# Two PSUM banks set apart for the gate products, smaller stores of the normalised rows, and an earlier start of two stages

## The chip, the core and the metric

The kernel runs on one core of one Trainium2 chip. The metric is the device time of one execution in microseconds (us). The profile comes from one more execution of the same program, taken by the hardware profiler; "unit", "slot" and "step" below are words of this kernel and are explained with it.

## What is computed

Eight sequences of 3008 tokens with 256 channels are filtered in the frequency domain (a real FFT along the tokens, a product with a complex filter, the inverse FFT). Each token is then normalised by its root mean square and goes through a SwiGLU feed-forward layer of width 1536:

```python
X = np.fft.rfft(x, axis=1)
y = np.fft.irfft(X * (filt_r + 1j * filt_i)[None], n=x.shape[1], axis=1)
t = y.reshape(8 * 3008, 256)
xn = t / np.sqrt(np.mean(t * t, axis=-1, keepdims=True) + 1e-6) * rms_g
g = xn @ w_gate
out = (g / (1 + np.exp(-g)) * (xn @ w_val)) @ w_out
```

## The kernel before

**The feed-forward layer** is the frame of the kernel. The tokens of a batch are cut into chunks (eight chunks of 376 tokens for batch 0, five of 512 and one of 448 for each of batches 1 to 7), and the hidden width into 12 tiles of 128. One chunk and one tile make a *unit*; there are 96 units for batch 0 and 72 for each later batch. `unit(g, jt)` multiplies the gate weights into the PSUM bank `pg` (L341, two matmuls) and the value weights into `pv` (L345, two matmuls), lets ScalarE write silu of `pg` to `sg` (L348), and lets VectorE write `pv` times `sg` to `hh` (L350). `project` follows three units behind and adds `hh` times the output weights to the two banks `po` of the chunk (L363), which are held for 12 units, then copied out and stored.

**The filter** of a batch runs in three steps that are inserted between the units by a plan written out by hand. `s1` is the first small Fourier product (bank `psa`, L144) and stores to the DRAM array `a_tmp`; `load_a2` reads it back in another order (L160). `s2` multiplies by the second table (bank `psp`, L200), and VectorE and GpSimd apply the filter (for batches 0 and 1 VectorE alone, tiles `t` at L207 and L208); `s2z` is the product back (bank `psz`, L229 and L232), copied by ScalarE to `z_sb` (L234) and stored to `z_tmp`; `load_z2` reads that back (L244). `s3` is the last product (bank `psy`, L250); ScalarE squares and sums each half of it (tile `junk`, L256), `s3r` makes the factor `rho` on GpSimd (L265, L267) one slot later, and `s3n` lets VectorE write the normalised rows to `n_sb` two slots after `s3` (L276), the last reader of `psy`. Four calls of `s3n` fill a tile that is stored to `n_tmp`; when a batch is stored, `load_xn` reads its chunks back transposed as `xn` (L318), which the units of that batch use.

Batch 0 goes ahead of the units. Its first product is turned on TensorE (`turn`, bank `psa`, L189, copied at L192), its normalised rows go by `s3n_first` (L287) and `load_xn_first`, and its first two chunks by `turn_n` (L299, L304, L306).

**The order.** `tc.manual_schedule()` keeps the order of the Python code on each engine. The main loop calls `unit(u)`, then the steps that the plan has for slot u, then `project` for unit u - 3:

```python
        for u in range(total + LAG):
            if u < total:
                unit(u // JT, u % JT)
                steps(u)
            if u >= LAG:
                project((u - LAG) // JT, (u - LAG) % JT)
```

Within a slot `s3n` and `s3n_first` come first, then `s3r`, then `s2z`, then the rest. For batch 1 `s2` starts in slot 14 with one call every three slots, `s2z` three slots behind it, and `s3` starts in slot 63 with two calls in every three slots. For batch b from 2 on `s3` starts 31 slots ahead of the batch's first unit, with four calls in every five slots. `s3` of batch 0's chunks 2 to 7 takes two slots in every eight from slot 2 to slot 43, and `s1` of batch 2 takes slots 44 to 59.

**PSUM.** All products use tiles of one bank from one pool of eight. A new tile takes a bank that is free in the program's order; its first matmul waits until the last reader of the bank's former tile is done.

**The queues.** Stores, and the loads of `a2`, `z2` and `xn`, are issued by SyncE's queue in the order of the code. `x` is loaded by GpSimd's queue.

Of the kernel before, what the change touches and what calls it, by code (L numbers as in the profile page):

```python
# [10 lines left out]
FP32 = mybir.dt.float32  # L11
FP16 = mybir.dt.float16
# [4 lines left out]
P = 128  # L17
D = 256
# [7 lines left out]
PY = 96  # L26
# [48 lines left out]
def kernel(  # L75
# [11 lines left out]
    nc = tc.nc  # L87
# [10 lines left out]
    n_dram = nc.dram_tensor("n_tmp", (B, PY, RP, D), FP16, kind="Internal").ap()  # L98
    n0_dram = nc.dram_tensor("n0_tmp", (RP // 4, PY, 4, D), FP16, kind="Internal").ap()

    glob = ctx.enter_context(tc.tile_pool(name="glob", bufs=1))
    work = ctx.enter_context(tc.tile_pool(name="work", bufs=2))
    psum = ctx.enter_context(tc.tile_pool(name="psum", bufs=8, space=bass.MemoryType.PSUM))

    def bank(name):
        return psum.tile([P, 512], FP32, tag="bank", name=name)

    w1_sb = glob.tile([PX, QZ], FP16)
    t_sb = glob.tile([QZ, PY], FP16)
# [29 lines left out]
    def s1(b, i, eng):  # L139
        v = st[b]  # L140
        if i % 4 == 0:
            v.a = work.tile([QZ, 8, D], FP16, tag="a_sb", name="a_sb", bufs=4)
        ps = bank("psa")
        nc.tensor.matmul(ps[0:QZ, :], w1_sb, v.x[i // 4][:, ds(2 * (i % 4), 2), :],  # L144
                         start=True, stop=True)
        dst = v.a[:, ds(2 * (i % 4), 2), :]
        src = ps[0:QZ, :].rearrange("p (r d) -> p r d", r=2)
        if eng == 0:
            nc.scalar.activation(out=dst, in_=src, func=AXT.Copy)  # L149
        else:  # L150
            nc.vector.tensor_copy(out=dst, in_=src)
        if i % 4 == 3:
            nc.sync.dma_start(
                a_dram[b].rearrange("s c r d -> (s c) r d")[:, ds(8 * (i // 4), 8), :], v.a)
# [8 lines left out]
    def s1_first(g):  # L163
        v = st[0]
        if g == 0:
            t1 = work.tile([P, RP, D], FP16, tag="z2", name="at", bufs=1)
            v.at = t1.rearrange("p a b -> p (a b)")[:, 0:2 * NS * P].rearrange(
                "p (h s r c) -> p h s r c", h=2, s=NS, r=RP)
            v.a2 = work.tile([P, NS, D], FP16, tag="a2", name="a2", bufs=1)
        for i in range(2):  # L170
            for dh in range(2):
                ps = bank("psa")
                for r in range(4):
                    nc.tensor.matmul(ps[:, ts(r, QZ)], v.x[g][:, 4 * i + r, ts(dh, P)], w1_sb,
                                     start=(r == 0), stop=(r == 3))
                dst = v.at[:, dh, :, ds(8 * g + 4 * i, 4), :]
                src = ps[:, 0:4 * QZ].rearrange("p (r s c) -> p s r c", r=4, s=NS)
                if dh == 0:
                    nc.scalar.activation(out=dst, in_=src, func=AXT.Copy)
                else:  # L180
                    nc.vector.tensor_copy(out=dst, in_=src)

    def turn(j):
        v = st[0]
        ps = bank("psa")
        for e in range(2):
            for dh in range(2):
                k = 2 * e + dh
                nc.tensor.matmul(ps[:, ts(k, P)],  # L189
                                 v.at[:, dh, 2 * j + e, :, :].rearrange("p r c -> p (r c)"),  # L190
                                 eye_sb, start=(k == 0), stop=(k == 3))
        nc.scalar.activation(out=v.a2[:, ts(j, 2), :],  # L192
                             in_=ps.rearrange("p (s d) -> p s d", s=2), func=AXT.Copy)
# [77 lines left out]
    def s3n(b, q):  # L271
        v = st[b]
        ps, rho = v.y.pop(q)
        if q % 4 == 0:
            v.n = work.tile([PY, 8, D], FP16, tag="n_sb", name="n_sb", bufs=2)
        nc.vector.tensor_tensor(out=v.n[:, ds(2 * (q % 4), 2), :],  # L276
                                in0=ps[0:PY, :].rearrange("p (r d) -> p r d", r=2),
                                in1=rho.unsqueeze(-1).to_broadcast([PY, 2, D]), op=ALU.mult)
        if q % 4 == 3:
            nc.sync.dma_start(n_dram[b, :, ds(8 * (q // 4), 8), :], v.n)  # L280

    def s3n_first(c):
        v = st[0]
        n = work.tile([PY, 8, D], FP16, tag="n_sb", name="n0", bufs=2)
        for k in range(2):
            ps, rho = v.y.pop(2 * c + k)
            nc.vector.tensor_tensor(out=n[:, ts(k, 2), :],  # L287
                                    in0=ps[0:PY, :].rearrange("p (r d) -> p r d", r=2),
                                    in1=rho.unsqueeze(-1).to_broadcast([PY, 2, D]), op=ALU.mult)
        if c >= PRE:  # L290
            nc.sync.dma_start(n0_dram[c], n[:, 0:4, :])
        return n

    def turn_n(c, n):
# [41 lines left out]
    def unit(g, jt):  # L336
        b, c, w = chunks[g]
        xn = st[b].xn[c]
        pg = bank("pg")
        for dt_ in range(2):  # L340
            nc.tensor.matmul(pg[:, 0:w], wg_sb[:, dt_, ts(jt, P)], xn[:, dt_, 0:w],  # L341
                             start=(dt_ == 0), stop=(dt_ == 1))
        pv = bank("pv")
        for dt_ in range(2):
            nc.tensor.matmul(pv[:, 0:w], wv_sb[:, dt_, ts(jt, P)], xn[:, dt_, 0:w],  # L345
                             start=(dt_ == 0), stop=(dt_ == 1))
        sg = work.tile([P, 512], FP32, tag="sg", name="sg", bufs=3)
        nc.scalar.activation(out=sg[:, 0:w], in_=pg[:, 0:w], func=AXT.Silu)  # L348
        hh = work.tile([P, 512], FP16, tag="hh", name="hh", bufs=5)
        nc.vector.tensor_tensor(out=hh[:, 0:w], in0=pv[:, 0:w], in1=sg[:, 0:w], op=ALU.mult)  # L350
        hh_of[(g, jt)] = hh
# [44 lines left out]
    def at(slot, f, *args):  # L396
        plan.setdefault(slot, []).append((f, args))

    for c in range(PRE, RP // 4):
        k = 2 + 8 * (c - PRE)  # L400
        at(k, s3, 0, 2 * c, 2)
        at(k + 1, s3, 0, 2 * c + 1, 2)
        at(k + 2, s3r, 0, 2 * c, 2)
        at(k + 4, s3n_first, c)
        at(k + 7, load_xn_first, c)

    for b in range(1, B):
        end = FIRST + UNITS * (b - 1)
        o_s1 = 44 if b == 2 else end - 118
        o_s2, p_s2 = (14, 3) if b == 1 else (end - 75, 2)  # L410
        o_s3 = 63 if b == 1 else end - 31
        if b > 1:
            at(o_s1 - 18, load_x, b)
            for i in range(16):
                at(o_s1 + i, s1, b, i, i % 2 if b == 2 else 0)
            at(o_s1 + 16, load_a2, b)
        for j in range(12):
            k = o_s2 + p_s2 * j
            at(k, s2, b, j)
            at(k + (3 if b < 2 else 5), s2z, b, j)  # L420
        at(k + (4 if b < 2 else 6), load_z2, b)
        for q in range(16):
            k = o_s3 + q + (q // 2 if b == 1 else q // 4)
            at(k, s3, b, q)
            at(k + 1, s3r, b, q)
            at(k + 2, s3n, b, q)
        for c in range(6):
            at(k + 3 + c, load_xn, b, c)
# [62 lines left out]
    with tc.manual_schedule():  # L491
# [20 lines left out]
        for j in range(15):  # L512
            if j < 12:
                turn(j)
            if 0 <= j - 2 < 12:
                s2(0, j - 2)
            if j in (2, 5, 8):
                copy_f(j // 3 + 1)
            if 0 <= j - 4 < 12:
                s2z(0, j - 4)  # L520
            if j == 6:
                load_w(4)
            if j == 10:
                load_x(1)
                for i in range(4):
                    fold_w(i, nc.gpsimd)
                load_wo(0)
# [12 lines left out]
        load_wo(1)  # L540
        load_wo(2)
        n0 = s3n_first(0)
        turn_n(0, n0)
        load_w(4)
        n1 = s3n_first(1)
        at(2, turn_n, 1, n1)
        load_z2(0, 16, 16)
# [5 lines left out]
# [6 lines that stand above are left out]
# [31 lines left out]
```

## Time and profile before

| | |
|---|---|
| median of 3 runs (lowest to highest) | 903.63 us (902.5 to 903.73) |
| the profiled execution's own time | 903.38 us |
| its span, first to last instruction | 901.5 us |
| granted TensorE clock, mean over the span | 0.984 |
| granted TensorE clock, first 50 us and next 50 us | 0.83 and 0.90 |
| granted TensorE clock from 100 to 850 us | 1.00 |
| ScalarE's `sg` (L348), x600 | 569 ns mean |
| VectorE's `hh` (L350), x600 | 658 ns mean |
| ScalarE's `junk` (L256), x256 | 380 ns mean, and 191 ns for reading the sum |
| VectorE's `n_sb` (L276), x112 | 677 ns mean |
| store of `n_tmp` from `n_sb`, x28 of 384 KB | 3.0 us median to landing |
| store of `n_tmp` from `n`, x6 of 192 KB | 2.5 us median to landing |
| load of `a`, x28 of 384 KB | 5.7 us median to landing |

Busy shares are averages over the span, and the ends of matmuls are modelled. So the distance from the start of one matmul to the start of the next says more about a delay on TensorE than its busy time does. In a line of the timeline the first number is the start in us from the span's start, the second is how long the row lasts; a line with "x2" holds two instructions in one. Idle time and what ended it stand in brackets. Instructions of different units overlap in a timeline, so a chain is read by going from each line to the one that it waits for.

### The profile page before, as it was taken

The page shows a single profiled execution, that of the slowest core. Times are in us where ns is not written, and L with a number is a line of the kernel's source. Part 1 is how long each engine was busy: PE and PEld are TensorE (multiplying, and loading weights), DVE is VectorE, ACT ScalarE, POOL GpSimd, SP SyncE. Part 2 cuts the span into 40 slices and gives each one's busy share as a digit, 9 for nine tenths or more (in the row PEclk, how much of TensorE's full clock was granted, in tenths as well). Part 3 has the DMA queues.
Part 4 walks back from the last instruction along what each step waited for, and adds up shares of the span by engine and source line. Part 5 has one row for each costly group of instructions (what it writes and reads, how often), then busy time and mean ns, then how long its engine had stood idle before and what let it go on. Part 6 is the DMA issues. An engine that isn't in the chain of part 4 may idle for free.

```text
span 901.5 us, 16399 instructions
## 1 busy us (share of the span) xinstructions
PE 864.4 (96%) x5528; PEld 549.9 (61%) x5528; DVE 647.1 (72%) x1025; ACT 641.4 (71%) x1455; POOL 336.7 (37%) x438
## 2 busy tenths in 40 slices
PE   5769999999999999999999999999999999999997
PEld 4436776666556655666556665566656665566655
DVE  4768887895588847797477965789477985865554
ACT  4656768677886778677886878867786775854543
POOL 3822104492245803285044821459033850500000
PEclk9869999999999999999999999999999999999999
DMA  8996665565435565344645554365653425260101
GB/s 201 243 261 149 162 163 187 119 147 140 136 101 142 127 146 170 99 109 129 161 147 129 141 126 143 107 131 144 146 159 100 96 78 116 77 130 24 43 29 45
DMA packets 140796, 117.30 MB, mean 130 GB/s; under 512 B 53960, under 2 KB 125256, under 8 KB 140712
## 3 DMA queue, kind: packets, MB, share of 16 engines
q1 hardware_dynamic: 136472, 102.36, 42.0%
q0 software_dynamic: 4240, 13.90, 8.6%
q8 instruction: 43, 0.70, 0.3%
q14 instruction: 41, 0.34, 0.1%
HBM read 56.96 MB, written 60.42 MB: 130 GB/s over the span
## 4 chain that ended last, share of the span: by engine, by line
PE 87%; ACT 4%; DMA 3%; DVE 2%; issue 2%; POOL 0%; SPq 0%; ACTq 0%; DVEq 0%; POOLq 0%
PE po L363 26%; PE pv L345 26%; PE pg L341 25%; PE psy L250 2%; PE psa L144 2%; ACT junk L256 2%; PE psp L200 2%; PE psz L229 2%; ACT sg L348 1%; DMA xt<-in_x_dram 1%; DMA z_tmp<-z_sb 1%; DVE t L208 1%; DMA z<-z_tmp 1%; PE psz L232 0%; DMA n_tmp<-n_sb 0%
## 5 line engine op out<-in xcount | busy, mean ns | idle before, releaser
L350 DVE TENSOR_TENSOR hh<-pv,sg 128x512 f16<-128x512 f32 (+2 forms) x600 | 393.5, 658 | 220.1 <-ACT sg L348 128.8
L348 ACT ACTIVATE sg<-pg 128x512 f32<-128x512 f32 (+2 forms) x600 | 341.3, 569 | 197.8 <-PE pg L341 164.2
L363 PE MATMUL po<-wo_sb,hh 128*128 128x256 f16 (+2 forms) x2304 | 350.0, 272 | 0.9 <-ACT xn L304 0.6
L345 PE MATMUL pv<-xn,wv_sb 128*128 128x512 f16 (+2 forms) x1200 | 342.5, 367 | 4.6 <-ACT sg L348 3.8
L341 PE MATMUL pg<-xn,wg_sb 128*128 128x512 f16 (+2 forms) x1200 | 342.7, 367 | 2.9 <-DMA xn<-n_tmp 1.7
L363 PEld LDWEIGHTS <-hh 128*128 128x128 f16 (+2 forms) x2304 | 235.0, 104 | 102.8 <-DVE n_sb L276 0.5
L345 PEld LDWEIGHTS <-wv_sb 128*128 128x128 f16 x1200 | 117.4, 98 | 133.2 <-issue 6.2
L265 POOL TENSOR_SCALAR me<-ms 96x2 f32<-96x2 f32 (+1 forms) x120 | 26.3, 219 | 346.2 <-ACT junk L256 339.3
L341 PEld LDWEIGHTS <-wg_sb 128*128 128x128 f16 x1200 | 117.3, 98 | 17.4 <-issue 2.6
L217 POOL TENSOR_TENSOR pi<-pi,fi_sb 64x512 f32<-64x512 f32 x72 | 91.4, 1269 | 71.0 <-ACT pi L214 67.5
L256 ACT ACTIVATE junk<-psy 96x256 f16<-96x256 f32 x256 | 97.2, 380 | 19.8 <-PE psy L250 7.8
L218 POOL TENSOR_TENSOR qq<-pr,pi 128x512 f16<-128x512 f32 x72 | 91.8, 1274 | 10.5 <-DVE pi L216 5.0
L267 POOL TENSOR_TENSOR rho<-me,half_sb 96x2 f32<-96x2 f32 (+1 forms) x120 | 87.7, 731 | 10.0
L276 DVE TENSOR_TENSOR n_sb<-psy,rho 96x512 f16<-96x512 f32 x112 | 75.8, 677 | 0.0
L234 ACT ACTIVATE z_sb<-psz 128x512 f16<-128x512 f32 x96 | 57.3, 597 | 10.1 <-PE psz L232 5.7
L149 ACT ACTIVATE a_sb<-psa 96x512 f16<-96x512 f32 x94 | 55.7, 592 | 7.1 <-PE psa L144 3.3
L250 PE MATMUL psy<-z,t_sb 96*96 96x512 f16 x128 | 49.2, 389 | 6.9 <-DMA z<-z_tmp 6.9
L216 DVE TENSOR_TENSOR pi<-psp,fi_sb 64x512 f32<-64x512 f32 x72 | 49.9, 693 | 1.9
L215 DVE TENSOR_TENSOR pr<-psp,fr_sb 128x512 f32<-128x512 f32 x72 | 49.7, 690 | 0.7
L256 ACT ACTIVATION_READ_ACCUMULATOR junk<-psy 96x1 f32 x256 | 49.0, 191 | 0.0
L214 ACT ACTIVATE pi<-psp 64x512 f32<-64x512 f32 x72 | 42.4, 589 | 6.1
L144 PE MATMUL psa<-xt,w_sb 94*96 94x512 f16 x112 | 43.8, 413 | 2.0 <-DMA xt<-in_x_dram 2.0
(53 smaller groups left out, 383.4 us busy)
## 6 DMA issues: line engine op xcount, KB each, us to landing
out_dram<-o SPq DMA_DIRECT2D x70, 256.0 KB, 2.5
z_tmp<-z_sb SPq DMA_DIRECT2D x32, 384.0 KB, 2.3
xt<-in_x_dram POOLq DMA_DIRECT2D x32, 376.0 KB, 7.2
a_tmp<-a_sb SPq DMA_DIRECT2D x28, 384.0 KB, 3.6
a<-a_tmp SPq DMA_DIRECT2D x28, 384.0 KB, 5.7
z<-z_tmp SPq DMA_DIRECT2D x7, 1536.0 KB, 10.1
n_tmp<-n_sb SPq DMA_DIRECT2D x28, 384.0 KB, 3.0
out_dram<-o SPq DMA_DIRECT2D x14, 224.0 KB, 2.6
```

The lines of the kernel that those rows point to most:

```text
L144: nc.tensor.matmul(ps[0:QZ, :], w1_sb, v.x[i // 4][:, ds(2 * (i % 4), 2), :], start=True, stop=True)
L217: nc.gpsimd.tensor_tensor(out=pi[64:P], in0=pi[64:P], in1=fi[64:P], op=ALU.mult)
L218: nc.gpsimd.tensor_tensor(out=qq, in0=pr, in1=pi, op=ALU.subtract)
L250: nc.tensor.matmul(ps[0:PY, :], t_sb, v.z2[:, ts(q, 2), :], start=True, stop=True)
L256: nc.scalar.activation(out=junk, in_=ps[0:PY, ts(i, D)], func=AXT.Square, scale=0.0625, accum_out=v.ms[:, ds(k + i, 1)])
L267: nc.gpsimd.tensor_tensor(out=rho, in0=me, in1=half_sb[:, 0:2 * pair], op=ALU.pow)
L276: nc.vector.tensor_tensor(out=v.n[:, ds(2 * (q % 4), 2), :], in0=ps[0:PY, :].rearrange("p (r d) -> p r d", r=2), in1=rho.unsqueeze(-1).to_ ...
L341: nc.tensor.matmul(pg[:, 0:w], wg_sb[:, dt_, ts(jt, P)], xn[:, dt_, 0:w], start=(dt_ == 0), stop=(dt_ == 1))
L345: nc.tensor.matmul(pv[:, 0:w], wv_sb[:, dt_, ts(jt, P)], xn[:, dt_, 0:w], start=(dt_ == 0), stop=(dt_ == 1))
L348: nc.scalar.activation(out=sg[:, 0:w], in_=pg[:, 0:w], func=AXT.Silu)
L350: nc.vector.tensor_tensor(out=hh[:, 0:w], in0=pv[:, 0:w], in1=sg[:, 0:w], op=ALU.mult)
L363: nc.tensor.matmul(po[0:n, ts(s4 % 2, D)], hh[:, ds(s4 * wb, n)], wo_sb[:, jt, :], start=(jt == 0 and s4 % 2 == 0), stop=(jt == JT - 1 and ...
```

## The change

The pool of eight banks becomes two rings by tag: two banks ("own") for `pg` and for the `psa` of `turn`, and six ("bank") for everything else, that is `pv`, `po`, `psp`, `psz`, `psy`, `psn`, `psv` and the `psa` of `s1` and `s1_first`. The tile of normalised rows holds four rows instead of eight, in four buffers instead of two, so a batch is stored in eight pieces of 192 KB instead of four of 384 KB; `s3n_first` uses tiles of the same new size. For batch 1, `s2` with `s2z` and `load_z2`, and `s3` with `s3r`, `s3n` and `load_xn`, all stand two slots earlier. The plan of the other batches is as it was.

```diff
-    def bank(name):
-        return psum.tile([P, 512], FP32, tag="bank", name=name)
+    def bank(name, own=False):
+        return psum.tile([P, 512], FP32, tag="own" if own else "bank", name=name,
+                         bufs=2 if own else 6)
...
     def turn(j):
         v = st[0]
-        ps = bank("psa")
+        ps = bank("psa", True)
...
     def s3n(b, q):
         v = st[b]
         ps, rho = v.y.pop(q)
-        if q % 4 == 0:
-            v.n = work.tile([PY, 8, D], FP16, tag="n_sb", name="n_sb", bufs=2)
-        nc.vector.tensor_tensor(out=v.n[:, ds(2 * (q % 4), 2), :],
+        if q % 2 == 0:
+            v.n = work.tile([PY, 4, D], FP16, tag="n_sb", name="n_sb", bufs=4)
+        nc.vector.tensor_tensor(out=v.n[:, ds(2 * (q % 2), 2), :],
...
-        if q % 4 == 3:
-            nc.sync.dma_start(n_dram[b, :, ds(8 * (q // 4), 8), :], v.n)
+        if q % 2 == 1:
+            nc.sync.dma_start(n_dram[b, :, ds(4 * (q // 2), 4), :], v.n)
...
     def s3n_first(c):
         v = st[0]
-        n = work.tile([PY, 8, D], FP16, tag="n_sb", name="n0", bufs=2)
+        n = work.tile([PY, 4, D], FP16, tag="n_sb", name="n0", bufs=4)
...
-            nc.sync.dma_start(n0_dram[c], n[:, 0:4, :])
+            nc.sync.dma_start(n0_dram[c], n)
...
     def unit(g, jt):
         b, c, w = chunks[g]
         xn = st[b].xn[c]
-        pg = bank("pg")
+        pg = bank("pg", True)
...
-        o_s2, p_s2 = (14, 3) if b == 1 else (end - 75, 2)
-        o_s3 = 63 if b == 1 else end - 31
+        o_s2, p_s2 = (12, 3) if b == 1 else (end - 75, 2)
+        o_s3 = 61 if b == 1 else end - 31
```

## The prediction

> **What bounds the kernel now.** I read the page's busy times first, then the windows by stage, TensorE's waits, and the timeline around each wait; beside it, the bank that the built program gives each tile. A bank's release lies 0.05 to 0.1 ahead of the end of each of today's waits named here, so the places say which waits come.
>
> ```profile
> PE 864.4 (96%) x5528; PEld 549.9 (61%) x5528; DVE 647.1 (72%) x1025; ACT 641.4 (71%) x1455; POOL 336.7 (37%) x438
> ```
>
> ```profile
> 57.00:175.00 118.00, 114.06 (x791) 78.76 (x790) 98.33 (x186) 85.07 (x240) 27.81 (x51) 0.99 0.64 161
> 175.00:280.60 105.60, 104.77 (x655) 65.38 (x656) 76.53 (x118) 81.49 (x182) 46.62 (x60) 1.00 0.55 139
> ```
>
> The two lower lines are stretches: from and to, length, then the busy us of PE, weight loads, VectorE (DVE), ScalarE (ACT) and GpSimd, the granted clock, the DMA share and GB/s. TensorE (PE) is the bound: 114.1 of 118 us in batch 0's units, 104.8 of 105.6 in a later batch. So an edit can win only what PE loses, and every new wait of PE is paid in full. PE's losses are where the start of one matmul is further from the last than its pitch (0.16 us for 376 columns, 0.21 for 512, 0.11 for 256). Over batch 0's units they are a few waits of 0.1 to 0.9 us, and one at the end:
>
> ```profile
> 175.08 0.61 PE L341 MATMUL pg<-xn,wg_sb 128*128 128x512 f16 x2 [1.68 <-DMA xn<-n_tmp]
> ```
>
> Batch 1's first `xn` comes late: the last matmul before it starts at 173.12, so 1.85 us are lost. A third kind comes five times, always 0.8 of idle time, as PE's waits count it:
>
> ```profile
> PE pv L345 <- ACT sg L348: 3.8, 5, 0.8
> ```
>
> This is the first of them, with the s3 steps of the batch that lead to it; the others follow every 105.5 us, up to 700 us:
>
> ```profile
> 253.53 0.38 PE L250 MATMUL psy<-z,t_sb 96*96 96x512 f16 x1
> ...
> 254.03 0.38 ACT L256 ACTIVATE junk<-psy 96x256 f16<-96x256 f32 x1
> ...
> 254.53 0.38 ACT L256 ACTIVATE junk<-psy 96x256 f16<-96x256 f32 x1
> ...
> 254.90 0.58 ACT L348 ACTIVATE sg<-pg 128x512 f32<-128x512 f32 x1
> ...
> 255.52 0.69 DVE L350 TENSOR_TENSOR hh<-pv,sg 128x512 f16<-128x512 f32 x1 [0.66 <-ACT sg L348]
> ...
> 256.12 0.68 DVE L276 TENSOR_TENSOR n_sb<-psy,rho 96x512 f16<-96x512 f32 x1
> ...
> 256.57 0.38 PE L250 MATMUL psy<-z,t_sb 96*96 96x512 f16 x1
> ...
> 257.22 0.59 PE L341 MATMUL pg<-xn,wg_sb 128*128 128x512 f16 x2
> ...
> 257.94 0.58 ACT L348 ACTIVATE sg<-pg 128x512 f32<-128x512 f32 x1
> ...
> 258.58 0.59 PE L345 MATMUL pv<-xn,wv_sb 128*128 128x512 f16 x2 [0.76 <-ACT sg L348]
> ```
>
> At the bottom `pv` sits in the bank of its own unit's `pg` (so the build places it) and starts 0.06 after `sg` ends (257.94 + 0.58), at 258.58 instead of 257.65: 0.93 lost. The upper lines are what counts for the change: a chain without slack from one `psy` to the `n_sb` that frees the `psy` before it.
>
> **Part 1: two banks for `pg`, six for the rest, in batches 2 to 7.** The losses of `pv` by `pg` go, 0.93 in each of five batches. `pg` itself is read 1.00 to 1.3 us after its start and its bank is wanted two units (2.6 us) later, so it costs nothing. But `po` holds two of the six, and `pv`, `psy`, `psp` and `psz` share four, where before they also drew on what `pg` left free. In the s3 stretch the changed build puts the fourth `psy` of each run of four units into the bank of the first. The chain above is what frees it: second `psy` 253.53, ..., `n_sb` of the first ends 256.12 + 0.68 = 256.80, 3.27 us. With 0.05 to start again the fourth `psy` can start 3.32 after the second; it starts 256.57 - 253.53 = 3.04 after it now. New stall 0.28, in each of the four runs of a batch. In the third run the second `psy` takes the bank of a `pv` whose `hh` ends at 253.66, after 253.53: 0.18 more. Together 4 x 0.28 + 0.18 = 1.30 a batch. Six batches pass s3 like that, the last one without such a loss now: 6 x 1.30 - 5 x 0.93 = +3.1. Bounds: 0 (chain 0.1 shorter and the 0.18 hidden) and +4.5 (0.05 more a run).
>
> **Part 2: the same in units 3 to 50.** Here s3 of batch 0 holds two `psy` for 5 to 8 us, s2 and s2z of batch 1 run, and VectorE works 98 of 118 us. Times from a bank's first matmul to its release, shortest in the trace: `pv` 1.27, `psz` 1.23, `psp` 1.71. By the changed build's places:
> - in units 21, 30, 36 and 45 `psp` takes the bank of the same unit's `pv`, which it follows by 0.32 (`pv`) + 0.43 (`psz`) = 0.75; 1.27 + 0.05 - 0.75 = 0.57, four times: 2.3.
> - at the chunk changes (15, 27, 39) the new `po` takes banks of `psy` and `psz` that are just being read: 0.7, 0.2, 0.7 by the same sums, 1.6.
> - units 45 and 46, where s1 joins in: `pv` behind `psa` and `psp`, `psa` behind `psa`: 1.2.
> - units 3 to 8: `pv` behind `pv` adds 0.87, of which 0.53 are waits that are there already: 0.3.
>
> The losses that PE has between units 12 and 50 now, by start distances, are 2.2, and go: 5.4 - 2.2 = +3.2. Bounds: 0 (the same crowding, only elsewhere) and +6 (`pv` lives of 1.6 to 2.0, which many of these units have).
>
> **Part 3: s2 two slots sooner.** s2 of batch 1 needs `a2`. Its last load:
>
> ```profile
> L160 SPq DMA_DIRECT2D a<-a_tmp x1: 1617/1617/1617, 67.6 to 67.6; - x1
> DMA to landing us min/median/max: 6.5/6.5/6.5
> ```
>
> ```profile
> 74.50 0.38 PE L200 MATMUL psp<-a,u_sb 128*128 128x256 f16 x2
> ```
>
> It lands at 74.17 and is used at 74.50, so 0.33 are to spare, and two slots here are 1.92. The first `psp` would come at 72.58, plus 0.3 from units 3 to 8; PE would stand at 74.2: +1.3. Nothing in the change moves the SP queue before it. Queued behind that matmul is all of PE. Bounds +0.3 (the units before are slower still) and +1.6.
>
> **Part 4: s3 and `load_xn` two slots sooner.** The load of `z2` lands 0.5 before its first use now (126.50 + 10.2 against 137.20), and both move by two slots, with two more s1 steps between: no stall. In slots 61 to 83 `psy` follows a `pv` of the unit before in its bank: `pv` lives 1.54 to 1.68 there and the distance is some 1.49, so 0.17 in each of eight groups, 1.4; losses there now 0.85: +0.6 (bounds 0 and +1.5). The `xn` wait: `n_sb` now ends 167.05, `xn` lands 8.0 later. Two units are 1.9, and the copies of `o`, which stand ahead of that `n_sb` now, then come behind it; the wait of 1.85 goes with some 0.7 to spare: -1.85 (bounds -1.85 and 0).
>
> **Part 5: stores in eight pieces.** 28 more DMAs on SP's queue of 0.33 us issue each, in stretches where SP waits for ScalarE and VectorE; a 192 KB store lands in 2.5 us against 3.0. The tile is reused after eight calls as before. Cost nothing; the cover is SP's idle time, and if it failed the 0.7 of spare for `xn` would be eaten first. The Trainium skill (Perfetto Trace Analysis, DMA Optimizations) says that batching small transfers from 2 KB to 4 KB raises throughput; the new runs are 2 KB, and by that rule the last store would be the slower one, which at worst leaves `xn` where part 4 has it less a few tenths.
>
> **Part 6: ahead of the units.** `turn` with two banks delays the third turn by 0.6, but VectorE's copy of the filter until 20.26 hides it. The third and fourth of the last four `psa` of s1 wait for copies (0.6 each) of the first two: +0.2 ahead of `n0` and all units (bounds 0 and 0.5).
>
> Sum: +3.1 + 3.2 + 1.3 + 0.6 - 1.85 + 0.2 = +6.55 on the profiled execution's 903.38 (span 901.5, 1.9 around it): 909.9. The median of the runs is 0.25 above that execution: 910.2.
>
> **Rivals.**
> - *Faster: the waits of `pv` on `sg` go and nothing takes their place.* For it: 0.93 a batch is a plain clash of places, and `xn` late is plain too. Against it: the 3.27 chain has no gap in it. It decides at 3.04 - 0.05: if the chain ends within 2.99, no run stalls. Then -4.65 (5 x 0.93), -1.85, -2.2 of units 12 to 50 and -0.85 of 61 to 83: 903.63 - 9.55 = 894.1. Chance 0.09.
> - *Units 3 to 50 crowd as before and `a2` is met:* parts 2 and 3 give nothing, +3.1 + 0.6 - 1.85 + 0.2 = +2.05 is left: 905.7. For it: a waiting PE lets VectorE catch up. Against: `psp` right behind `pv` can't be caught up. Chance 0.13.
> - *The clock falls.* The granted clock was 1.00 through gaps of 0.93 and 1.85 us here, which speaks against it; the first units (57.2 to 60.4) ran at half pitch, so one such fall costs 1.6 us, and 24 runs of s3 would cost 38: 942 without the forecast's waits. The Trainium skill (TensorE: Matmul & The Clock Gate, A second HAM failure mode: psum-queue depth-cycling) describes a kernel whose clock swung because PE idled briefly between groups while it cycled through banks. By that rule this rival holds; the trace shows no such swing. Chance 0.03.
> - That the change doesn't do what it says: the earlier s2 is void where PE only waits for `a2`; that is in the sum.
>
> **How the numbers follow.** Forecast 0.75, rivals 0.09, 0.13 and 0.03. A measurement of this kernel tells about 0.2%, 1.8 us, from no change. The forecast's low bounds reach into that with 0.02; the second rival lies in it with 0.05, above with 0.07, below with 0.01; the first is faster. Faster 0.10, same 0.07, slower 0.83. The range of 904.3 to 914.7 leaves out the first and third rival, the lower part of the second, and the ends of the forecast where parts 1 and 2 are both at a bound (0.05).
>
> **What would show it.** Right: in the waits of PE, `psy` on DVE `n_sb` four times a batch near 0.28, `pv` on `sg` gone, `psp` on `hh` and on DMA `a` in batch 0's units, no wait for `xn`; batches 2 to 6 take 105.9 us instead of 105.5. Wrong: batches at 104.6 us, or 57 to 175 us shorter than now by more than the `xn` wait.

## The result and the profile after

| | before | after |
|---|---|---|
| median of 4 runs (lowest to highest) | 903.14 us (902.5 to 903.73) | 914.35 us (913.4 to 915.72) |
| the profiled execution's own time, and its span | 903.38, 901.5 | 914.52, 912.6 |
| granted TensorE clock, mean over the span | 0.984 | 0.986 |

The ratio is 1.0126, with an interval of 1.0113 to 1.0139: slower by 11.2 us. Line numbers of the changed kernel are one higher than those of before from `bank` on (`pg` L342, `pv` L346, `po` L364, `psy` L251, `psp` L201, `hh` L351, `sg` L349, `n_sb` L277).

Busy times of the page after:

```profile
PE 874.0 (96%) x5528; PEld 547.5 (60%) x5528; DVE 647.0 (71%) x1025; ACT 640.9 (70%) x1455; POOL 336.8 (37%) x438
```

These engines run as many instructions as before; what is new is that the span is 11 us longer. TensorE even *reads* 9.6 us busier than before (874.0 against 864.4) with the same 5528 matmuls, and `pg`, `pv` and `po` last 367, 367 and 272 ns in the mean in both kernels. So a part of its waiting is booked as work. The rows of matmuls overlap: one of 512 columns lasts 0.38 us, and the next starts some 0.22 after it. A start that is up to 0.16 late shortens the overlap and leaves no idle time. The stretches show the same. The first is 118 us of batch 0's units, the other two are two later batches. Columns are as in the prediction.

```profile
56.82:175.00 118.18, 110.21 (x743) 74.30 (x743) 93.47 (x175) 80.38 (x231) 24.71 (x48) 0.98 0.62 153
181.50:287.38 105.88, 105.86 (x656) 64.91 (x653) 77.74 (x121) 81.57 (x183) 47.93 (x61) 1.00 0.56 140
287.38:393.41 106.03, 106.02 (x658) 65.32 (x656) 77.68 (x119) 81.67 (x183) 47.37 (x61) 1.00 0.52 134
```

The 72 units of the third line took this before:

```profile
280.28:385.79 105.51, 104.75 (x658) 65.59 (x656) 77.76 (x119) 81.58 (x183) 47.42 (x61) 1.00 0.52 135
```

The batch takes 106.03 us, 0.52 more than before, and TensorE is busy for 106.02 of it: by this line nothing is lost. The clock is 1.00. So from here on a loss is measured as in the prediction, by the distance between the starts of matmuls. Summed over stretches of units (from the first gate matmul of one unit to that of the next stretch), the change against the kernel before in the two profiled executions is:

| units | 0-12 | 12-13 | 13-51 | 51-88 | 88-96 | 96-528 | 528-end | sum from unit 0 |
|---|---|---|---|---|---|---|---|---|
| after, us | +1.00 | +1.73 | +3.17 | +2.96 | -2.02 | +4.47 | +0.24 | +11.55 |

Ahead of unit 0 it was -0.41. A step that moves from one stretch to another takes its matmuls with it: the first `s2` of batch 1 (two matmuls, 0.22 us) stood in unit 14 before and stands in unit 12 now. So 0.22 of the +1.73 is work and no wait, and units 13 to 51 lose 3.39 by waits.

Of TensorE's waits after, over the whole run, these are the five largest that the kernel before does not have (total, times, longest):

```profile
PE psp L201 <- DMA a<-a_tmp: 1.3, 1, 1.3
PE psp L201 <- DVE hh L351: 1.3, 3, 0.6
PE po L364 <- DVE o L380: 1.3, 2, 0.6
PE pv L346 <- DVE hh L351: 1.1, 3, 0.5
PE psy L251 <- DVE hh L351: 1.1, 5, 0.3
```

The five waits of `pv` on `sg` and the wait for `xn` are gone. What came in their place, apart from the wait for `a`, are waits for the *six* banks. Here are two of them in the timeline. `psp` in the bank of its own unit's `pv`:

```profile
97.78 0.48 PE L346 MATMUL pv<-xn,wv_sb 128*128 128x376 f16 x2
...
98.49 0.55 DVE L351 TENSOR_TENSOR hh<-pv,sg 128x376 f16<-128x376 f32 x1 [0.47 <-ACT sg L349]
...
99.09 0.38 PE L201 MATMUL psp<-a,u_sb 128*128 128x256 f16 x2 [0.40 <-DVE hh L351]
```

`pv` starts at 97.78, its reader `hh` ends at 98.49 + 0.55 = 99.04, and `psp` starts 0.05 later; without the wait it would have started 0.75 after `pv`, at 98.53, so 0.56 are lost. And this is the end of one of the four runs of s3 of a later batch:

```profile
247.35 0.69 DVE L351 TENSOR_TENSOR hh<-pv,sg 128x512 f16<-128x512 f32 x1 [0.66 <-ACT sg L349]
...
247.53 0.59 PE L342 MATMUL pg<-xn,wg_sb 128*128 128x512 f16 x2
...
247.96 0.68 DVE L277 TENSOR_TENSOR n_sb<-psy,rho 96x512 f16<-96x512 f32 x1
248.09 0.59 PE L346 MATMUL pv<-xn,wv_sb 128*128 128x512 f16 x2
...
248.69 0.38 PE L251 MATMUL psy<-z,t_sb 96*96 96x512 f16 x1
```

The fourth `psy` waits for the `n_sb` that ends at 247.96 + 0.68 = 248.64. No bracket stands behind any of TensorE's rows, but `pv` starts 0.56 after `pg` and `psy` 0.60 after `pv`, where two 512-column matmuls take 0.43: 0.13 and 0.17 lost. The wait at `pv` is one for a bank as well, by its time: `pv` starts 0.05 after the `hh` of the unit before ends (247.35 + 0.69 = 248.04). VectorE does this `hh` and the `n_sb` one behind the other, so the end of `n_sb` sets the whole loss. All 24 runs of s3 (four in each of six batches) show both: `pv` 0.05 behind `hh` and `psy` 0.05 to 0.06 behind `n_sb`. The start of one unit to the next is 1.81 in place of 1.52.

### The profile page after: what moved, and what is told of

Its sections match the earlier page's. It is cut to its first block, busy times and chain, and to the rows that moved or that the text cites. A ratio compares the mean times of both kernels' runs of the same rounds, so it can differ in the third digit from the quotient of the medians.

```text
span 912.6 us, 16480 instructions
## 1 busy us (share of the span) xinstructions
PE 874.0 (96%) x5528; PEld 547.5 (60%) x5528; DVE 647.0 (71%) x1025; ACT 640.9 (70%) x1455; POOL 336.8 (37%) x438
## 4 chain that ended last, share of the span: by engine, by line
PE 88%; DMA 4%; DVE 3%; ACT 2%; issue 1%; POOL 1%; SPq 1%; ACTq 0%; DVEq 0%; POOLq 0%
PE po L364 26%; PE pv L346 26%; PE pg L342 25%; PE psy L251 4%; PE psa L145 2%; PE psp L201 2%; PE psz L230 2%; DMA fi_sb<-in_filt_i_dram 1%; ACT junk L257 1%; DVE hh L351 1%; DMA z_tmp<-z_sb 1%; DMA a<-a_tmp 1%; DVE t L209 1%; ACT sg L349 1%; SPq L161 1%
## 5 line engine op out<-in xcount | busy, mean ns | idle before, releaser
L351 DVE TENSOR_TENSOR hh<-pv,sg 128x512 f16<-128x512 f32 (+2 forms) x600 | 393.4, 658 | 227.2 <-ACT sg L349 138.5
L349 ACT ACTIVATE sg<-pg 128x512 f32<-128x512 f32 (+2 forms) x600 | 341.1, 569 | 196.3 <-PE pg L342 158.5
L364 PE MATMUL po<-wo_sb,hh 128*128 128x256 f16 (+2 forms) x2304 | 350.1, 272 | 2.2 <-DVE o L380 1.3
L346 PE MATMUL pv<-xn,wv_sb 128*128 128x512 f16 (+2 forms) x1200 | 342.6, 367 | 1.5 <-DVE hh L351 1.1
L342 PE MATMUL pg<-xn,wg_sb 128*128 128x512 f16 (+2 forms) x1200 | 342.5, 367 | 0.8 <-ACT xn L305 0.8
L364 PEld LDWEIGHTS <-hh 128*128 128x128 f16 (+2 forms) x2304 | 235.6, 104 | 105.7 <-issue 6.7
L346 PEld LDWEIGHTS <-wv_sb 128*128 128x128 f16 x1200 | 117.3, 98 | 132.4 <-issue 8.8
L342 PEld LDWEIGHTS <-wg_sb 128*128 128x128 f16 x1200 | 117.3, 98 | 15.3 <-issue 3.5
L277 DVE TENSOR_TENSOR n_sb<-psy,rho 96x512 f16<-96x512 f32 x112 | 75.8, 677 | 0.0
L235 ACT ACTIVATE z_sb<-psz 128x512 f16<-128x512 f32 x96 | 57.3, 597 | 11.1 <-PE psz L233 6.5
L251 PE MATMUL psy<-z,t_sb 96*96 96x512 f16 x128 | 49.9, 395 | 8.2 <-DMA z<-z_tmp 7.1
```

What stands on the lines that cost most here:

```text
L251: nc.tensor.matmul(ps[0:PY, :], t_sb, v.z2[:, ts(q, 2), :], start=True, stop=True)
L277: nc.vector.tensor_tensor(out=v.n[:, ds(2 * (q % 2), 2), :], in0=ps[0:PY, :].rearrange("p (r d) -> p r d", r=2), in1=rho.unsqueeze(-1).to_ ...
L364: nc.tensor.matmul(po[0:n, ts(s4 % 2, D)], hh[:, ds(s4 * wb, n)], wo_sb[:, jt, :], start=(jt == 0 and s4 % 2 == 0), stop=(jt == JT - 1 and ...
```

## The experiments

All kernels compute the full reference. "By stretch" means the table at the end of this section, which is made like the one above.

**1. The two rings alone** (tiles of eight rows and the old slots):

```diff
-        return psum.tile([P, 512], FP32, tag="bank", name=name)
+        return psum.tile([P, 512], FP32, tag="own" if own else "bank", name=name,
+                         bufs=2 if own else 6)
...
     def turn(j):
...
-        ps = bank("psa")
+        ps = bank("psa", True)
...
     def unit(g, jt):
...
-        pg = bank("pg")
+        pg = bank("pg", True)
```

> The kernel before with the two rings of banks alone (two and six), tiles of eight rows and the old slots. If the ring of six is the cause (the theory): batches 2 to 7 lose 4.3 us as in the changed kernel, units 3 to 50 some 4, units 60 to 88 some 2.5, and the wait for xn of 1.85 stays: 912 to 915 us, with no wait of psp on the load of a. If the earlier slots of batch 1 are the cause of the loss in batch 0's units (the rival): 906 to 908.

Measured: 915.39 us, ratio 1.0141 (1.0125 to 1.0156). The rings alone cost 12 us; the rest of the change gives about one back. By stretch the later batches lose 4.11, units 13 to 51 lose 4.87. The waits of TensorE from 55 us on show one thing the theory did not have:

```profile
PE psp L201 <- DVE hh L351: 2.5, 5, 0.6
...
PE pg L342 <- DMA xn<-n_tmp: 0.5, 1, 0.5
```

The wait for `xn` is down to 0.5 of idle time from 1.7 with nothing moved: TensorE itself comes later to it. The unit before it starts 8.6 us later than in the kernel before, and the last `n_sb` of the batch ends 8.1 later.

**2. The earlier slots alone** (one ring of eight):

```diff
-        o_s2, p_s2 = (14, 3) if b == 1 else (end - 75, 2)
-        o_s3 = 63 if b == 1 else end - 31
+        o_s2, p_s2 = (12, 3) if b == 1 else (end - 75, 2)
+        o_s3 = 61 if b == 1 else end - 31
```

> The kernel before with batch 1's steps two slots sooner alone, one ring of eight. The theory: the xn wait of 1.85 us goes, psp waits for the load of a for 1.3 to 1.5 in unit 12, the rest is as before: 902 to 903.5 us. The rival, that the earlier slots fall badly onto batch 0's own steps: 905 to 907.

Measured: 902.82 us, ratio 0.9991 (0.9979 to 1.0004), no difference that can be told. The waits from 55 us on:

```profile
PE pv L345 <- ACT sg L348: 3.8, 5, 0.8
PE psp L200 <- DMA a<-a_tmp: 1.6, 1, 1.6
```

The `xn` wait is gone, the wait for `a` has come, and the five `pv` waits stay, as they belong to the banks. By stretch: +1.95 at `a`, -1.10 in units 13 to 51, +0.60 in units 51 to 88, -2.02 at `xn`. The first two hold the 0.22 of the moved `s2`, so 0.88 of the 1.10 are waits that went, most of them around unit 16 (the first `s2` shared slot 14 with an `s3n_first` before, and no longer does).

**3. The eight pieces alone** (`s3n_first` with its tile `n0` changed alike):

```diff
-        if q % 4 == 0:
-            v.n = work.tile([PY, 8, D], FP16, tag="n_sb", name="n_sb", bufs=2)
+        if q % 2 == 0:
+            v.n = work.tile([PY, 4, D], FP16, tag="n_sb", name="n_sb", bufs=4)
...
-            nc.sync.dma_start(n_dram[b, :, ds(8 * (q // 4), 8), :], v.n)
+            nc.sync.dma_start(n_dram[b, :, ds(4 * (q // 2), 4), :], v.n)
```

> The kernel before with n stored in eight pieces alone. The theory: the last store of batch 1 is shorter by 0.5 us, and the xn wait with it, the rest as before: 902.5 to 903.2 us. The rival, that 28 more stores hold up SP's queue: 904 or more, with PE waiting for DMAs.

Measured: 902.61 us, ratio 0.9995 (0.9984 to 1.0006). DMA issues of this kernel (kind, number, size, median us to landing):

```profile
n_tmp<-n_sb SPq DMA_DIRECT2D x56, 192.0 KB, 2.1
```

A store of 192 KB lands in 2.1 us where the one of 384 KB took 3.0, and the `xn` wait is shorter by 0.40 by stretch. The 28 extra issues on SyncE's queue cost nothing that can be seen.

**4. The chain of s3 cut shorter, in the changed kernel.** `s3n` comes one unit after `s3` instead of two, in batches 2 to 7; within the slot `s3r` stands ahead of it:

```diff
-            at(k + 2, s3n, b, q)
+            at(k + (1 if b > 1 else 2), s3n, b, q)
...
-    ORDER = {s3n: 0, s3n_first: 0, s3r: 1, s2z: 2}
+    ORDER = {s3r: 0, s3n: 1, s3n_first: 1, s2z: 2}
```

> The changed kernel with the normalising step of batches 2 to 7 one slot after s3 instead of two (after s3r in the same slot), so that psy is released a unit sooner. If the chain from psy to the n_sb that frees the psy before it makes the stalls of s3 (the theory): the four stalls of 0.3 in each batch go, and the changed kernel's +4.3 us in batches 2 to 7 becomes 0 to -4.6: 905.5 to 910 us. If six banks are too few whatever the chain is (the rival): stalls go on at pv and psp, 913 to 915.

Measured: 905.28 us, ratio 1.0027 (1.0015 to 1.0038). The 72 units that took 106.03 us in the changed kernel:

```profile
286.06:390.66 104.60, 104.60 (x659) 65.57 (x657) 78.11 (x119) 81.76 (x183) 47.43 (x61) 1.00 0.52 136
```

They take 104.60. In the s3 stretch around 247 us all units with a `psy` take 1.52 or less, but for the first, which takes 1.74 in the kernel before and the changed one too. The changed kernel has four at 1.81 to 1.84 and two at 1.59 and 1.63. So each batch lost 1.43 to the late release of `psy`: the edit moves only `s3n` with its stores, and `s3r` within its slot. It does change which banks the later tiles get, as experiment 5 will show; what ties the loss to this chain is that `pv` and `psy` start right behind `hh` and `n_sb` in all 24 runs. The banks stay divided, and in batches 2 to 7 this kernel is 4.42 *faster* than before.

**5. The same in the kernel before** (one ring of eight).

> The kernel before, one ring of eight banks, with the normalising step of batches 2 to 7 one slot after s3 instead of two. In the changed kernel this step alone took 0.92 us off each of five batches more than the four stalls of s3, so the theory is that a psy held for one unit less is what matters for either layout: the wait of pv on sg, 0.93 in each of five batches, goes, and nothing else moves: 898.5 to 899 us. The rival, that only a ring of its own keeps pv out of pg's bank: 903, with the five waits still there.

Measured: 900.59 us, ratio 0.9971 (0.9959 to 0.9984). That is a gain, but half of the one expected. The waits and the timeline of this kernel:

```profile
PE psy L250 <- ACT sg L348: 1.6, 5, 0.3
```

```profile
255.22 0.58 ACT L348 ACTIVATE sg<-pg 128x512 f32<-128x512 f32 x1
...
255.86 0.38 PE L250 MATMUL psy<-z,t_sb 96*96 96x512 f16 x1 [0.33 <-ACT sg L348]
```

The five `pv` waits of 0.93 are gone, and a `psy` now falls into the bank of the `pg` just ahead of it: 0.49 by start distance, once in each of five batches. With one ring, moving one release shifts later tiles to other banks, and a new clash of places came up.

**6. The best of the parts on one ring:** the pieces, `s3n` one unit behind `s3` from batch 1 on, and s3 of batch 1 from slot 63 with three calls in every four slots (`q // 3` in place of `q // 2`), so that it ends sooner without starting sooner. Beside the diff of 3 and the `ORDER` of 4:

```diff
-            k = o_s3 + q + (q // 2 if b == 1 else q // 4)
+            k = o_s3 + q + (q // 3 if b == 1 else q // 4)
...
-            at(k + 2, s3n, b, q)
+            at(k + 1, s3n, b, q)
```

> A version meant to beat both: one ring of eight banks, n in eight pieces, the normalising step one slot after s3 in all batches from 1 on, and batch 1's s3 with three calls in every four slots from slot 63 (so that its last call is in slot 83 instead of 85) while s2 stays where it was. The theory: -4.65 from the five waits of pv and -1.85 from xn, no wait on the load of a: 896.5 to 898 us. The rival, that the denser s3 of batch 1 makes ScalarE the bound there: 898.5 or more, with waits on sg between units 63 and 84.

Measured: 900.23 us, ratio 0.9967 (0.9954 to 0.998). The same `psy` on `sg`, 1.6 of idle time in five batches, holds it back; `xn` is no longer waited for. The time is that of the rival, but not for its reason: these waits stand in s3 of batches 2 to 6 and not between units 63 and 84.

**7. Experiment 4 with `s3n` one unit behind `s3` in batch 1 as well:**

```diff
-            at(k + (1 if b > 1 else 2), s3n, b, q)
+            at(k + 1, s3n, b, q)
```

> The changed kernel with the normalising step one slot after s3 in batch 1 too. If the 3.0 us that units 60 to 88 lose come from psy being held too long in six banks (the theory): about 2 of them go, 903 to 904 us. If they come from VectorE's copies of o at the chunk changes (the rival): 905, with po still waiting for o by 1.3.

Measured: 903.13 us, ratio 1.0007 (0.9997 to 1.0016), no different from before. Units 51 to 88 lose 1.27 instead of 2.96. What is left there are two waits of `po`:

```profile
PE po L364 <- ACT sg L349: 1.2, 2, 0.6
```

They stand at units 63 and 75 and cost 0.75 each by start distance. The view puts them down to ScalarE; in the changed kernel `po` waits for VectorE's copy there. Which reader frees the bank in this kernel was not looked into.

**8. `psp` of batch 1 into the ring of `pg`,** in the changed kernel:

```diff
-        ps = bank("psp")
+        ps = bank("psp", b == 1)
```

> The changed kernel with psp of batch 1 in the ring of two beside pg instead of the ring of six. If psp in the bank of its own unit's pv makes the loss of units 13 to 51 (the theory): its waits on hh (1.3 idle, 0.57 each by start distances) go, units 13 to 51 lose 1 to 1.5 instead of 3.2 and pg doesn't wait: 912 to 912.8 us. The rival, that six banks are short there in any case or that pg now waits for psp: 914 or more.

Measured: 913.6 us (911.46 to 915.63), ratio 1.0111 (1.0089 to 1.0133). By the medians it can't be told from the change itself. By stretch it can: units 13 to 51 lose 1.76 instead of 3.17. The three waits of `psp` on `hh` are gone from the list, and `psp` waits once for `pg`'s reader instead:

```profile
PE psp L201 <- ACT sg L349: 0.5, 1, 0.5
```

The gain shows in its stretch and not in the total, whose four runs lie 4.2 us apart; the profiled execution began unit 0 2.2 us later than that of the change.

**9 to 11. Versions to beat both kernels.** Number 9 is number 6 with s2 of batch 1 from slot 15 and s3 from slot 64, number 10 is the changed kernel with `psp` in `pg`'s ring, `s3n` one unit behind `s3` from batch 1 on and the slots 14 and 63 with `q // 3`. Number 11 is number 9 with s3 from slot 65. Against number 6, for 9 and 11:

```diff
-        o_s2, p_s2 = (14, 3) if b == 1 else (end - 75, 2)
-        o_s3 = 63 if b == 1 else end - 31
+        o_s2, p_s2 = (15, 3) if b == 1 else (end - 75, 2)
+        o_s3 = 64 if b == 1 else end - 31    # 65 in number 11
```

> The version best1 with batch 1's s2 from slot 15 and its s3 from slot 64, a slot later than in best1, so that the first s2 no longer meets batch 0's normalising step in slot 14. The theory: the waits around units 14 to 17 (1.56 us by start distances) shrink by about 1, the load of a is met with 1.3 to spare, xn keeps its room: 0.5 to 1.2 us below best1. The rival, that z2 or the chunk changes make up for it: equal to best1 within 0.3.

Measured: 899.1 us, ratio 0.9955 (0.9942 to 0.9967). With s2 one slot later units 13 to 51 stand at -1.10 as in experiment 2, but 0.44 of this are the matmuls of the last `s2z`, which moved on into unit 51; 0.66 are waits that went. s3 then comes before its input:

```profile
PE psy L250 <- DMA z<-z_tmp: 1.3, 1, 1.3
```

> The changed kernel's two rings with what the other runs showed to help them: psp of batch 1 beside pg, the normalising step one slot after s3 in batches 1 to 7, batch 1's s2 back in slot 14, its s3 from slot 63 with three calls in four slots. The theory that six banks suffice wherever psy is released a unit sooner, and are short only in batch 0's units: batches 2 to 7 gain 4.4 us as in after_s3n1, units 13 to 88 lose some 3, the xn wait is gone: 900.5 to 902 us, no better than best1. The rival, that the rings are as good as one ring once psy goes early: 898 to 899.5.

Measured: 901.09 us, ratio 0.9977 (0.9967 to 0.9987). With the chain of s3 and `psp` mended the divided banks beat the kernel before too, but not number 9 on one ring (899.1, measured together with it).

> The version best2 with batch 1's s3 from slot 65 instead of 64, since in best2 the first psy waits 1.3 us for the load of z2. The theory: that wait shrinks to 0.3, xn is still in time (its last row comes one slot sooner than in the kernel before, from a shorter store): 1 us below best2, 898 us. The rival, that xn comes late instead: equal to best2, with PE waiting for xn.

Measured: 899.28 us, ratio 0.9955 (0.9941 to 0.9968). The wait for `z` is no longer in the list (units 51 to 88 at +0.53 instead of +2.04), and from unit 0 on it is 1.4 us shorter than number 9, but the medians are equal; its profiled execution began unit 0 1.3 us later. These two are the fastest versions found, 0.45% below the kernel before and 1.7% below the changed one.

Difference to the kernel before by stretch of units, one profiled execution each, us:

| kernel | ahead of unit 0 | 0-12 | 12-13 | 13-51 | 51-88 | 88-96 | 96-528 |
|---|---|---|---|---|---|---|---|
| after | -0.41 | 1.00 | 1.73 | 3.17 | 2.96 | -2.02 | 4.47 |
| 1 rings alone | -1.01 | 1.10 | 0 | 4.87 | 3.81 | -1.35 | 4.11 |
| 2 slots alone | -1.55 | 0.48 | 1.95 | -1.10 | 0.60 | -2.02 | -0.01 |
| 3 pieces alone | -0.24 | 0.53 | 0 | 0 | 0.23 | -0.40 | 0 |
| 4 after, `s3n` sooner | 0.35 | 0.98 | 1.05 | 3.18 | 3.00 | -2.03 | -4.42 |
| 5 before, `s3n` sooner | -1.36 | 0.49 | 0 | 0 | 0 | -0.33 | -2.16 |
| 6 parts on one ring | 0.66 | 0.51 | 0 | 0 | 0.13 | -2.02 | -2.17 |
| 7 as 4, batch 1 too | 1.27 | 1.09 | 1.75 | 3.18 | 1.27 | -2.02 | -4.43 |
| 8 `psp` beside `pg` | 1.76 | 1.08 | 0.91 | 1.76 | 2.96 | -2.03 | 4.47 |
| 9 | -0.14 | 0.27 | 0 | -1.10 | 2.04 | -2.01 | -2.19 |
| 10 | 0.59 | 1.09 | 0 | 2.59 | 1.00 | -2.02 | -4.42 |
| 11 | 1.18 | 0.38 | 0 | -1.11 | 0.53 | -2.03 | -2.19 |

## Why the prediction was right, and where its terms were off

The time lies inside the range, 4.1 us above the forecast of 910.2 and 0.35 below the upper end; one of the four runs, 915.72, lies beyond it. So there is luck in it that the range held: the loss of units 51 to 88 left its own bounds (2.96 against 0 to 1.5), and that of batches 2 to 7 came out at the edge of its own (4.47 against 4.5). The direction and the mechanism held: the six shared banks make TensorE wait for more than the two set apart save, and every such wait is paid in full. The sum was +6.55 and 11.1 was measured between the two profiled executions. Term by term:

**Batches 2 to 7: +3.1 forecast, +4.47 measured.** In the batch around 247 us the four runs lose 0.29, 0.32, 0.50 and 0.32, by the distance from unit to unit less the same units of experiment 4. The third run carries the extra 0.18 that was forecast (0.07 and 0.11 in its two earlier units). Each run loses 0.31 rather than 0.28, in all 1.43 a batch against 1.30. The five batches that save a `pv` wait took 0.67 and four times 0.52 longer than before, against 1.30 - 0.93 = 0.37 forecast. The one that had no `pv` wait to save lost 1.72: in its last run the `hh` of the unit before and the `n_sb` behind it end later, so that `pv` comes 0.41 late and `psy` 0.17 more. Experiment 4 shows the cause: with the release of `psy` one unit sooner the whole loss goes. The rival in which nothing takes the place of the `pv` waits is out by the same rows.

**Units 12 to 51: +2.9 forecast, +3.17 measured, 3.39 of it waits.** The new waits were put at 5.4, of which 0.3 belong to units 3 to 8, so at 5.1 from unit 12 on, less 2.2 that would go. By the distances between starts the chunk changes cost 1.6 and units 45 and 46 (without `psp`) 1.2, both as forecast. The four `psp`, with the `psz` ahead of them, cost 2.7 where 2.3 was forecast. They are not alike: the one shown above, in unit 30, loses the 0.57 that was worked out for each, but the one in unit 36 loses 1.2 and the one in unit 45 0.4. Experiment 1 has the same stretch at 4.87, with five waits of `psp` on `hh` instead of three and without the 1.10 by which the earlier slots shorten the stretch in experiment 2. Experiment 8 takes 1.41 off by moving `psp` alone. The rival in which these units crowd as before is out: TensorE that waits gave nothing back.

**Units 0 to 12: +0.3 forecast, +1.0 measured.** About half of that is no effect of the banks: kernels with the old banks have +0.27 to +0.53 there. The six with the divided banks have 0.98 to 1.10, so the rings are worth about 0.6.

**`a`: +1.3 forecast, +1.51 measured** by start distance (1.73 in its stretch, with the 0.22 of moved matmuls).

```profile
74.68 0.38 PE L201 MATMUL psp<-a,u_sb 128*128 128x256 f16 x2 [1.35 <-DMA a<-a_tmp]
```

The bracket has 1.35 of it. `a` landed 0.4 later than before, at 74.55. Experiment 2 shows the wait apart from the banks (+1.95, with the same 0.22).

**Units 51 to 88: +0.6 forecast, +2.96 measured. This is the step that failed.** It has two parts. First, a size: `psy` in the bank of the `pv` of the unit before was given 1.49 of distance. But that `psy` is the first of its pair, and the unit between has no `psy` of its own, so the distance is 1.28, and with a release after 1.6 the loss is 1.6 + 0.05 - 1.28 = 0.37 and not 0.17:

```profile
147.01 0.48 PE L346 MATMUL pv<-xn,wv_sb 128*128 128x376 f16 x2
...
148.04 0.55 DVE L351 TENSOR_TENSOR hh<-pv,sg 128x376 f16<-128x376 f32 x1 [0.68 <-ACT sg L349]
...
148.65 0.38 PE L251 MATMUL psy<-z,t_sb 96*96 96x512 f16 x1 [0.19 <-DVE hh L351]
```

From 147.01 to 148.65 it is 1.64; five such groups of the eight lose 0.36 to 0.42, though only some 0.2 of each stands in the list of waits. That makes 1.9 where 1.4 was forecast. Second, an omission: the chunk changes were counted up to unit 39 only. At units 63 and 75 the new `po` takes the bank of the old `po`, which ScalarE and VectorE copy out one after the other:

```profile
143.16 0.38 PE L364 MATMUL po<-wo_sb,hh 128*128 128x256 f16 x2
...
143.30 0.37 ACT L378 ACTIVATE o<-po 128x256 f32<-128x256 f32 x1
...
143.70 0.76 DVE L380 COPY o<-po 128x256 f32<-128x256 f32 x2 [0.59 <-ACT o L378]
...
144.18 0.27 PE L364 MATMUL po<-wo_sb,hh 128*120 128x256 f16 x1 [0.64 <-DVE o L380]
```

TensorE waits 0.64 here for VectorE's copy, and VectorE had waited 0.59 for ScalarE's. By start distance each of the two costs 0.80, in all 1.6 that the sum had at nothing. With the 1.9, and less some 0.6 of waits that went, this is the 2.96. Experiment 7 separates the parts: `s3n` one unit sooner in batch 1 takes 1.69 off, and two waits of `po` stay.

**`xn`: -1.85 forecast, -1.84 measured** (-2.02 with the rest of its stretch). **Pieces: 0 forecast, no difference that can be told,** experiment 3. Nor did the last store of batch 1 become the slower one: it landed 3.4 us after its issue there, against 3.9 before. **Ahead of the units: +0.2 forecast, -0.41 measured,** which says nothing, as the last section shows.

**The clock** stayed at 1.00 in the mean from 100 to 850 us, through gaps of 0.13 to 0.64 us, so the third rival is out. The Trainium skill (TensorE: Matmul & The Clock Gate, A second HAM failure mode: psum-queue depth-cycling) describes a kernel that cycles through banks and whose clock swings from brief idle times; the later stretches shown here, all at 1.00, have no such swing.

**What was to show it** was right for `psp`, `a`, `pv` and `xn`, and the batch was put at 105.9 us and took 106.03. It was wrong that `psy` on `n_sb` would stand in TensorE's list of waits: it is not there. The Trainium skill (Perfetto Trace Analysis, Optimization Strategy) says that the same gap repeated on the engine that should be saturated can mean that PSUM or SBUF is too small for the next tile. That agrees with what happens here, four times a batch, with one limit: the gaps are not to be seen as idle time, only in the starts.

## What to carry to other kernels

To divide a pool of banks, count for each kind of tile how long it lives and how many come in that time: what is set apart for one kind is taken from all others, and here the kind that got its own banks had not been the scarce one while `psy` was held so long. With `psy` released a unit sooner the division does pay in batches 2 to 7, by 4.42 us against 2.16 without it (experiments 4 and 5), and still loses more in batch 0's units. Before dividing banks look for the reader that frees one late: moving `s3n` up by one unit was worth 9.1 us in the divided kernel (914.35 to 905.28) and 2.4 in the undivided one, where the division alone cost 12. A step moved earlier to end one wait reaches its own input sooner, so look up how much that input has to spare (0.33 us for `a`, 0.5 for `z` here).

## What was not expected of the hardware

A short wait of TensorE does not show as one: 0.29 us per run of s3 falls into 0.13 at `pv` and 0.17 at `psy`, no row carries it, and TensorE reads busy 106.02 of 106.03 us while 1.43 of them are lost. Longer waits show too short by the same 0.16 or 0.17 by which rows overlap (0.40 for a loss of 0.56, 0.64 for 0.80, 0.19 for 0.36). The whole loss appears in the starts of matmuls and in the length of the stretch.

The stage ahead of the units is not the same length from one execution to the next: unit 0 began between 55.7 and 59.0 us in the profiled executions, also in kernels whose code up to there is the same as that of before. That is as much as several of the parts here are worth, and why experiments 8 and 11 are read by stretch. What sets it was not looked into and stays open.
